# Where the memory's product is read out of PSUM, and when a group's result is split, in an attention and mixture-of-experts kernel

## The chip, the core and the metric

The kernel runs on one core of a Trainium2 chip. The metric is the device time of one execution in microseconds (us). A core has five engines that run their own instruction streams and meet only at semaphores: TensorE (PE, with its weight loads shown as PEld), VectorE (DVE), ScalarE (ACT), GpSimd (POOL) and SyncE (SP, which here only issues transfers). Each engine works through its stream strictly in order.

## The reference

Three stages follow each other. The first is causal attention mixed with a linear memory, for 2 batches, 8 heads, 576 positions and 64 columns a head:

```
local   = softmax(q k' / 8, causal) v
phi(x)  = where(x > 0, x, exp(x) - 1) + 1
mem_out = (phi(q) M_prev) / (phi(q) z_prev + 1e-6)
attn    = g * mem_out + (1 - g) * local          # g = sigmoid(beta), one number a head
```

The second is a gated feed-forward layer, `(silu(x w_gate) * (x w_val)) w_out`, with 1152 tokens, 512 columns and 1536 inner columns. The third routes each token to one of 8 experts by the largest logit and puts it through that expert's two matrices with a ReLU between them. Everything is float32.

## The kernel before

**Precision.** Large products are made of three TensorE passes: each operand is kept as a high part (type fp32r, a copy with fewer bits) and a low part (the operand minus the high part). For the attention's result y, the high part `xh` is a cast by ScalarE and the low part `xl` a subtraction by GpSimd.

**Attention in 16 groups.** A group is one batch, one half of the positions (the first 256 or the last 320) and one pair of heads. In this text they are numbered 0 to 15 in the order in which they run: 0 to 3 are the first halves of batch 0, 4 to 7 its second halves, 8 to 15 the same for batch 1. A group has 2 or 3 units, each of 128 (or 64) query rows; there are 40 units. For a unit TensorE makes the scores (`emit_s`, into a PSUM tile of tag `s`), VectorE takes the row maximum (`emit_max`), ScalarE the exponentials P with their sums (`emit_exp`), TensorE transposes P (`emit_t`, tiles `tp`), ScalarE copies the transposes to SBUF (`PT`), and TensorE multiplies them with v into the group's PSUM tile `u` (`emit_av`).

**The end of a group** is in `emit_av` (lines 315 to 334). The weights of the softmax, (1 - g) over its sums, come from GpSimd as `rb`, are transposed into a PSUM tile `tr` and copied by ScalarE to `R` (line 275). TensorE makes the memory's product `mo` (line 329) from `ph`, which already holds g phi(q) over its norm. Then VectorE multiplies u with R (line 331) and adds mo, read from PSUM (line 332), ScalarE casts the sum to `xh` (line 333), and GpSimd subtracts for `xl` (line 334).

**Order.** The program is written out by hand: unit k+3 has its scores made while unit k is transposed and unit k-1 multiplied with v. One round of that is three ticks, 3k, 3k+1 and 3k+2; `emit_av` for a unit u runs in tick 3u+5. Other work hangs on ticks in a table (`at_tick`, run by `do`): loads, the phi(q) steps (`phi_exp`, `phi_sum`, `phi_norm`, `phi_t`), the scaling of q (lines 116 and 118), the repacking of the weights from 64-bit words (`narrow`, lines 422 to 427). From the fifth group on, after each tick a part of the feed-forward layer's first products is put in (`up`, tiles `gv`, line 492), with its weight splits (`wh` by ScalarE, line 453; `wl` by VectorE or GpSimd, line 456). That work fills TensorE where attention would leave it waiting.

**PSUM.** Three banks of tag `m` go round in turn among `tp`, `tr`, `tphi` (the transposes of phi(q)), `gv` and `mo` (the function `bank`). The fourth tile after `tr`, `mo` or any of them waits until the last reader of the first one is done.

Of the kernel before, what the change touches and what calls it, by code (L numbers as in the profile page):

```python
# [8 lines left out]
F32 = mybir.dt.float32  # L9
# [10 lines left out]
B, H, S, D = 2, 8, 576, 64  # L20
# [25 lines left out]
def tile_attention_moe(  # L46
# [18 lines left out]
    nc = tc.nc  # L65
# [4 lines left out]
    def pool(name, side=None, **kw):  # L70
        st = ExitStack()
        if side:
            kw["side"] = side
        return st.enter_context(tc.tile_pool(name=name, bufs=1, **kw)), st
# [8 lines left out]
    def bank(name):  # L83
        return psb.tile([128, 512], F32, tag="m", bufs=3, name=name)
# [5 lines left out]
    at, at_st = pool("at", "right")  # L90


    HALF = 256
# [3 lines left out]
    def cols(n):  # L97

        e = groups[n][1]
        return (HALF, S - HALF, S) if e else (0, HALF, HALF)  # L100
# [87 lines left out]
    NU = len(units)  # L188
# [14 lines left out]
    def emit_s(u):  # L203
        n, i = units[u]
        o, m = QT[i]
        w = o + m
        s = psa.tile([128, 2, 512], F32, tag="s", bufs=2, name="s")
        s_t[u] = s
        heads = [op_t[n][64 * h:64 * h + 64] for h in range(2)]
        if i < 4:  # L210
            for h, t in enumerate(heads):
                nc.tensor.matmul(s[:, h, 0:w], lhsT=t[:, 0, o:w], rhs=t[:, 1, 0:w], start=True, stop=False)  # L212
            for h in range(2):
                nc.tensor.matmul(s[:, h, o:w], lhsT=identb, rhs=maskb, start=False, stop=True)  # L214
        else:
            c = S // 2
            for a in range(2):
                for h, t in enumerate(heads):
                    nc.tensor.matmul(s[64 * h:64 * h + 64, a, 0:c], lhsT=t[:, 0, o:w], rhs=t[:, 1, a * c:a * c + c],
                                     start=True, stop=(a == 0), skip_group_check=True)  # L220
            nc.tensor.matmul(s[:, 1, c - 64:c], lhsT=identb, rhs=maskb2, start=False, stop=True, skip_group_check=True)
# [3 lines left out]
    def emit_max(u):  # L225
        n, i = units[u]
        P = at.tile([128, 2, 512], F32, tag="P", bufs=T["Pb"], name="P")
        st = at.tile([128, 2], F32, tag="st", bufs=5, name="st")
        sv, vs = views(u, s_t[u], P)
        k = len(vs)  # L230
        nc.vector.tensor_reduce(out=st[:, 0:k], in_=sv, axis=AX.X if k == 2 else AX.XY, op=ALU.max, negate=True)  # L231
        p_t[u] = (P, st, vs)
# [11 lines left out]
    def last_of(u):  # L244
        return u + 1 == NU or units[u + 1][0] != units[u][0]

    def emit_norm(u):

        if not last_of(u):
            return  # L250
        n, i = units[u]
        b, e, p = groups[n]
        k = 4 + e
        sm = sum_t.pop(n)[:, 0:k]
        nc.vector.tensor_scalar(sm, sm, 1e-9, None, op0=ALU.add)
        nc.vector.reciprocal(sm, sm)
        rb = r_t[n] = at.tile([128, 5, 64], F32, tag="rb", bufs=2, name="rb")
        nc.gpsimd.tensor_tensor(out=rb[:, 0:k], in0=sm.unsqueeze(2).to_broadcast([128, k, 64]),
                                in1=omgs[:, p, 0:k].unsqueeze(2).to_broadcast([128, k, 64]), op=ALU.mult)

    def emit_r(n):

        b, e, p = groups[n]
        rb, gw = r_t[n], cols(n)[1]
        t = bank("tr")
        for x in range(2):
            nc.tensor.transpose(out=t[:, 128 * x:128 * x + 128], in_=rb[:, 2 * x:2 * x + 2].rearrange("p a d -> p (a d)"),
                                identity=ident)
        if e:
            for h in range(2):  # L270
                hs_ = slice(64 * h, 64 * h + 64)
                nc.tensor.matmul(t[hs_, 256:320], lhsT=rb[hs_, 4], rhs=ident[hs_, hs_], start=True, stop=True,
                                 skip_group_check=True)
        R = r_t[n] = at.tile([128, S - HALF], F32, tag="R", bufs=2, name="R")
        nc.scalar.copy(R[:, 0:gw], t[:, 0:gw])

    def emit_t(u, x):

        n, i = units[u]
        P = p_t[u][0]  # L280
        if x == 0:
            pt_t[u] = at.tile([128, 2, 512], F32, tag="PT", bufs=2, name="PT")
        PT = pt_t[u]
        t = bank("tp")
        mode = T["ev" + str(0 if u < first[NP] else 1 if u < first[2 * NP] else 2)]
        ev = (nc.scalar.copy, nc.vector.tensor_copy)[(x % 2, 0, 1, x % 2 * (u % 2))[mode]]
        tv = t.rearrange("p (j m) -> p j m", m=128)
        if i < 4:
            for j in range(i + 1):
                nc.tensor.transpose(out=tv[:, j, :], in_=P[:, x, j * 128:(j + 1) * 128], identity=ident)  # L290
            ev(PT[:, x, 0:128 * (i + 1)], t[:, 0:128 * (i + 1)])  # L291
        else:
            pf, ptf = (z.rearrange("p a b -> p (a b)") for z in (P, PT))
            for y, j in enumerate(((0, 1, 2), (3, 4))[x]):
                kw = QT[j][1]
                nc.tensor.transpose(out=tv[0:kw, y, :], in_=pf[:, j * 128:j * 128 + kw], identity=ident)
            if x == 0:
                ev(ptf[:, 0:384], t[:, 0:384])
            else:
                ev(ptf[:, 384:512], t[:, 0:128])  # L300
                ev(ptf[0:64, 512:640], t[0:64, 128:256])

    def emit_av(u):
        n, i = units[u]
        vt = v_t[n]
        o, m = QT[i]
        PT = pt_t.pop(u)
        p_t.pop(u)
        ptf = PT.rearrange("p a b -> p (a b)")
        g0, gw, _ = cols(n)  # L310
        if u == first[n]:
            u_t[n] = psb.tile([128, 512], F32, tag="u", bufs=1, name="u")
        U = u_t[n]
        c0 = o - g0
        end = last_of(u)
        if end:
            emit_r(n)
        for j in range(i + 1):
            kw = QT[j][1]
            for h in range(2):  # L320
                rhs = PT[:, h, j * m:j * m + m] if i < 4 else ptf[0:kw, j * 128 + 64 * h:j * 128 + 64 * h + 64]
                nc.tensor.matmul(U[64 * h:64 * h + 64, c0:c0 + m], lhsT=vt[0:kw, j, 64 * h:64 * h + 64],  # L322
                                 rhs=rhs, start=(j == 0 and u == first[n]), stop=(end and j == i), skip_group_check=True)
        if end:
            b, e, p = groups[n]
            zt, mt, ph = batch_t[b]
            U, gs = u_t.pop(n)[:, 0:gw], slice(g0, g0 + gw)
            M = bank("mo")[:, 0:gw]
            nc.tensor.matmul(M, lhsT=mt[:, p, :], rhs=ph[e][:, p, :], start=True, stop=True)
            y = at.tile([128, S - HALF], F32, tag="y", bufs=2, name="y")[:, 0:gw]  # L330
            nc.vector.tensor_mul(y, U, r_t.pop(n)[:, 0:gw])  # L331
            nc.vector.tensor_add(y, M, y)  # L332
            nc.scalar.copy(xh[b][:, p, gs], y)
            nc.gpsimd.tensor_sub(xl[b][:, p, gs], y, xh[b][:, p, gs].bitcast(F32))

    chores = {}

    def at_tick(t, fn, *args):
        chores.setdefault(t, []).append((fn, args))

    def do(t):
        for fn, args in chores.pop(t, ()):
            fn(*args)
# [22 lines left out]
    def attn():  # L366
        for t in range(min(chores), -3 * LA):
            do(t)
        for k in range(-LA, NU + 1):
            do(3 * k)  # L370
            if k + LA < NU:
                emit_s(k + LA)
                emit_max(k + LA)
            if 0 <= k < NU:
                emit_t(k, 0)
            yield 3 * k
            do(3 * k + 1)
            if 0 <= k + LA - 1 < NU:
                emit_norm(k + LA - 1)
            if k + LA < NU:  # L380
                emit_exp(k + LA)
            if 0 <= k < NU:
                emit_t(k, 1)
            yield 3 * k + 1
            do(3 * k + 2)
            if 0 <= k - 1:
                emit_av(k - 1)
            yield 3 * k + 2


    WN = 2 * KC * 128
# [9 lines left out]
    for k, f in enumerate(seq):  # L401
        if f not in hold:
# [3 lines left out]
            y = max((y for y in range(RS) if k == 0 or hold[y] != seq[k - 1]), key=later)  # L406
# [114 lines left out]
    xh = [xw.tile([128, KC, S], F32R, name=f"xh{b}") for b in range(B)]  # L521
    xl = [xw.tile([128, KC, S], F32R, name=f"xl{b}") for b in range(B)]
# [83 lines left out]
    def bank2(name):  # L606
        return psc.tile([128, 512], F32, tag="c", bufs=4, name=name)
# [253 lines left out]
    for t in range(NT):  # L861
# [4 lines left out]
        y = bank2("y")  # L866
# [352 lines left out]
```

## Time and profile before

| | us |
|---|---|
| Runs of the kernel | 551.59, 553.46, 553.57 (median 553.46) |
| Profiled execution | 554.45 |
| Its span, first to last instruction | 552.7 |
| TensorE busy in the span | 520.3 (94%) |
| VectorE busy | 360.9 (65%) |
| ScalarE busy | 278.8 (50%) |
| GpSimd busy | 195.7 (35%) |

Attention with its filling takes the first 222 us or so of the span, the rest of the gated layer and the routing the stretch to about 400 us, and the experts what follows. TensorE's granted clock is full throughout. The share of busy time of an engine is a mean over these stages, so the rows below are cut by stretch. A busy TensorE is not TensorE at its peak, since its ends are modelled; its idle time is what the argument uses.

### The profile page before, as it was taken

How to read it: one execution, taken by the hardware profiler on the slowest of the kernel's cores; microseconds unless marked ns; L12 is line 12 of the kernel's file. 1: busy time of each engine (PE TensorE's matmuls, PEld its weight loads, DVE VectorE, ACT ScalarE, POOL GpSimd, SP SyncE). 2: the span in 40 equal slices, each digit the busy share in tenths (PEclk: the TensorE clock that was granted, in tenths of full speed). 3: DMA queues.
4: the chain of work that ended last, by engine and by line, in shares of the span. 5: the costliest groups of instructions: out<-in, count | busy, mean ns of one | idle time of the engine just before them, and what ended most of it. 6: DMA issues, size and time to landing. Idle time of an engine off the chain costs nothing. (4 is left out here: it accounts for less than half of the span.)

```text
span 552.7 us, 9638 instructions
## 1 busy us (share of the span) xinstructions
PE 520.3 (94%) x3497; PEld 428.4 (78%) x3497; DVE 360.9 (65%) x718; ACT 278.8 (50%) x623; POOL 195.7 (35%) x231
## 2 busy tenths in 40 slices
PE   4889998999989999999999999999989999989995
PEld 2545776887767889999999887778767979878774
DVE  5786877467876632687877486976688571818161
ACT  5668665565645542333353234434698553626361
POOL 3756356445632211222223475863323111010310
PEclk9999999999999999999999999999999999999999
DMA  8677383318640110699981325255699773554520
GB/s 271 225 244 251 134 268 132 94 49 297 207 157 2 39 39 2 180 283 283 275 256 36 120 74 232 95 156 175 219 341 339 281 254 138 167 211 162 189 90 6
DMA packets 43005, 96.33 MB, mean 174 GB/s; under 512 B 4598, under 2 KB 15350, under 8 KB 41408
## 3 DMA queue, kind: packets, MB, share of 16 engines
q1 hardware_dynamic: 41184, 91.04, 50.6%
q0 software_dynamic: 1760, 4.50, 2.2%
q8 instruction: 36, 0.59, 0.4%
q14 instruction: 25, 0.20, 0.1%
HBM read 78.68 MB, written 17.72 MB: 174 GB/s over the span
## 5 line engine op out<-in xcount | busy, mean ns | idle before, releaser
L492 PE MATMUL gv<-xh,wh 128*128 128x256 f32 (+1 forms) x384 | 122.6, 319 | 1.1 <-ACT PT L291 0.9
L492 PE MATMUL gv<-xh,wl 128*128 128x256 f32 (+1 forms) x384 | 113.8, 296 | 0.7 <-POOL wl L456 0.4
L492 PE MATMUL gv<-xl,wh 128*128 128x256 f32 (+1 forms) x384 | 113.5, 295 | 0.0
L492 PEld LDWEIGHTS gv<-xh,wh 128*128 128x128 f32 x384 | 72.7, 189 | 5.5 <-issue 3.1
L492 PEld LDWEIGHTS gv<-xh,wl 128*128 128x128 f32 x384 | 72.6, 189 | 1.3 <-POOL wl L456 0.8
L492 PEld LDWEIGHTS gv<-xl,wh 128*128 128x128 f32 x384 | 72.9, 190 | 0.7
L456 POOL TENSOR_TENSOR wl<-wf,wh 128x512 fp32r<-128x512 f32 x27 | 40.0, 1481 | 76.1 <-ACT wh L453 76.1
L1087 POOL DMA_INDIRECT out_dram<-hT,gi x13 | 15.5, 1191 | 121.9 <-ACT hT L1086 97.4
L231 DVE TENSOR_REDUCE st<-s 128x2 f32<-128x256 f32 (+4 forms) x40 | 32.2, 806 | 22.3 <-PE s L214 18.2
L241 ACT ACTIVATE P<-s,st 128x128 f32<-128x128 f32 (+4 forms) x72 | 39.2, 551 | 10.3 <-DVE st L231 9.9
L508 DVE SCALAR_TENSOR_TENSOR th<-th,gv 128x256 f32<-128x256 f32 (+1 forms) x48 | 21.7, 451 | 33.4 <-ACT th L507 33.3
L869 PE MATMUL y<-wo_h,hh 128*128 128x512 f32 x108 | 43.2, 400 | 0.0
L730 DVE SCALAR_TENSOR_TENSOR prod<-y,wrb 128x512 f32<-128x512 f32 x56 | 34.8, 686 | 11.9 <-ACT xr L727 11.9
L869 PE MATMUL y<-wo_h,hl 128*128 128x512 f32 x108 | 42.4, 392 | 0.0
L869 PE MATMUL y<-wo_l,hh 128*128 128x512 f32 x108 | 42.4, 392 | 0.0
L453 ACT CAST wh<-wf 128x512 fp32r<-128x512 f32 x54 | 33.6, 622 | 15.4 <-DMA wf<-wsp 15.4
L291 ACT COPY PT<-tp 128x128 f32<-128x128 f32 (+3 forms) x64 | 27.2, 426 | 27.9 <-PE tp L290 27.9
L212 PE MATMUL s<-qk 64*128 64x128 f32 (+3 forms) x128 | 28.5, 524 | 8.0 <-ACT qk L116 7.8
L1067 DVE SCALAR_TENSOR_TENSOR hcl<-w,hch 128x288 fp32r<-128x288 f32 x24 | 11.0, 457 | 35.5 <-ACT hch L1066 35.5
L322 PE MATMUL u<-PT,vt 128*64 128x128 f32 (+1 forms) x480 | 32.8, 269 | 0.3 <-DVE y L331 0.3
L630 POOL TENSOR_TENSOR hl<-hT,hh 128x512 fp32r<-128x512 f32 (+1 forms) x27 | 30.9, 1176 | 3.3 <-ACT hh L628 3.3
L290 PE MATMUL tp<-ident,P 128*128 128x128 f32 x160 | 28.1, 284 | 3.5 <-DVE y L332 1.4
(381 smaller groups left out, 1260.0 us busy)
## 6 DMA issues: line engine op xcount, KB each, us to landing
hT<-in_w_dram SPq DMA_DIRECT2D x64, 512.0 KB, 5.7
wr<-in_wgv_dram SPq DMA_DIRECT2D x12, 1024.0 KB, 5.9
wf<-wsp SPq DMA_DIRECT2D x15, 512.0 KB, 6.6
wor<-in_w_out_dram SPq DMA_DIRECT2D x12, 512.0 KB, 4.5
wsp<-wf SPq DMA_DIRECT2D x10, 512.0 KB, 6.7
disp<-pad SPq DMA_DIRECT2D x16, 257.0 KB, 7.0
xd<-disp SPq DMA_DIRECT2D x14, 257.0 KB, 6.4
qk<-in_qk_dram SPq DMA_DIRECT2D x8, 320.0 KB, 4.3
```

What stands on the lines that cost most here:

```text
L212: nc.tensor.matmul(s[:, h, 0:w], lhsT=t[:, 0, o:w], rhs=t[:, 1, 0:w], start=True, stop=False)
L231: nc.vector.tensor_reduce(out=st[:, 0:k], in_=sv, axis=AX.X if k == 2 else AX.XY, op=ALU.max, negate=True)
L241: nc.scalar.activation(o, a, AF.Exp, bias=st[:, x:x + 1], accum_out=sum_t[n][:, c + x:c + x + 1])
L290: nc.tensor.transpose(out=tv[:, j, :], in_=P[:, x, j * 128:(j + 1) * 128], identity=ident)
L291: ev(PT[:, x, 0:128 * (i + 1)], t[:, 0:128 * (i + 1)])
L322: nc.tensor.matmul(U[64 * h:64 * h + 64, c0:c0 + m], lhsT=vt[0:kw, j, 64 * h:64 * h + 64], rhs=rhs, start=(j == 0 and u == first[n]), stop ...
L453: nc.scalar.copy(hi[:, sl], w[:, sl])
L456: (nc.gpsimd if pool_ else nc.vector).tensor_sub(lo[:, sl], w[:, sl], hi[:, sl].bitcast(F32))
L492: nc.tensor.matmul(a, lhsT=wt[:, s, c, :], rhs=xt[b][:, c, sl], start=(c == 0 and y == 0), stop=(c == KC - 1 and y == 2))
L630: (nc.gpsimd if t else nc.vector).tensor_sub(hl[:, fs, d], src, hh[:, fs, d].bitcast(F32))
L730: nc.vector.scalar_tensor_tensor(out=prod[e % 2], in0=y, scalar=1.0, in1=wrb[e], op0=ALU.mult, op1=ALU.mult, accum_out=lg[:, e:e + 1])
L869: nc.tensor.matmul(y, lhsT=a[:, k, :], rhs=w[:, k, :], start=st, stop=en)
```

## The change

ScalarE copies `mo` from PSUM to a new SBUF tile `Ms` (two buffers) right behind the product, and VectorE's addition reads `Ms` in place of the PSUM tile. The cast to `xh` and the subtraction for `xl` leave `emit_av` and become a function of their own, `emit_xs`, hung on the table at the next tick, 3u+6. A last call of `do` runs that of the last group.

```
             M = bank("mo")[:, 0:gw]
             nc.tensor.matmul(M, lhsT=mt[:, p, :], rhs=ph[e][:, p, :], start=True, stop=True)
+            Ms = at.tile([128, S - HALF], F32, tag="Ms", bufs=2, name="Ms")[:, 0:gw]
+            nc.scalar.copy(Ms, M)
             y = at.tile([128, S - HALF], F32, tag="y", bufs=2, name="y")[:, 0:gw]
             nc.vector.tensor_mul(y, U, r_t.pop(n)[:, 0:gw])
-            nc.vector.tensor_add(y, M, y)
-            nc.scalar.copy(xh[b][:, p, gs], y)
-            nc.gpsimd.tensor_sub(xl[b][:, p, gs], y, xh[b][:, p, gs].bitcast(F32))
+            nc.vector.tensor_add(y, Ms, y)
+            at_tick(3 * u + 6, emit_xs, b, p, gs, y)
+
+    def emit_xs(b, p, gs, y):
+
+        nc.scalar.copy(xh[b][:, p, gs], y)
+        nc.gpsimd.tensor_sub(xl[b][:, p, gs], y, xh[b][:, p, gs].bitcast(F32))
...
             yield 3 * k + 2
+        do(3 * NU + 3)
```

The lines of the changed kernel behind this place stand up to 7 higher than before (453 is 460 there). The orders of TensorE, VectorE and SyncE are the same as before; those of ScalarE and GpSimd change. In the pieces below a number behind a name is the program's buffer: 86 is batch 0's `xh`, 81 and 84 are weight buffers.

ScalarE's stream at the end of group 6, before:

```order
L275 COPY R<-tr 128x320
L333 CAST xh_86<-y 128x320
L453 CAST wh_84<-wf_81 128x512
L151 ACTIVATE pe<-px 128x512
L152 ACTIVATE px<-px 128x512
L291 COPY PT<-tp 128x512
```

and of the changed kernel at the same place:

```order
L275 COPY R<-tr 128x320
L331 COPY Ms<-mo 128x320
L460 CAST wh_84<-wf_81 128x512
L151 ACTIVATE pe<-px 128x512
L152 ACTIVATE px<-px 128x512
L339 CAST xh_86<-y 128x320
L291 COPY PT<-tp 128x512
```

The cast to `xh` has moved behind a weight split and both phi(q) activations, and still stands ahead of the copy of the next transposes. Groups 5, 9, 11, 14 and 15 move it behind one or two other instructions in the same way.

ScalarE's stream at the end of group 0, before:

```order
L275 COPY R<-tr 128x256
L333 CAST xh_86<-y 128x256
L291 COPY PT<-tp 128x256
L241 ACTIVATE P,sums<-s,st 128x128 x2
L291 COPY PT<-tp 128x256
```

and of the changed kernel:

```order
L275 COPY R<-tr 128x256
L331 COPY Ms<-mo 128x256
L339 CAST xh_86<-y 128x256
L291 COPY PT<-tp 128x256
L241 ACTIVATE P,sums<-s,st 128x128 x2
```

Here nothing is written between the two ticks, so the cast stays where it was, behind the new copy. That is so in 10 of the 16 groups.

## Rows read from the trace of the kernel before

**Rows 1.** Busy time in stretches: stretch, length, then each engine's busy us (instructions)
```profile
30.00:45.00 15.00, 12.25 (x86) 6.41 (x84) 12.78 (x22) 10.27 (x30) 10.14 (x8) 1.00 0.70 223
...
60.00:75.00 15.00, 15.00 (x136) 11.69 (x138) 11.37 (x18) 8.09 (x22) 6.16 (x5) 1.00 0.66 209
75.00:90.00 15.00, 13.55 (x134) 10.85 (x131) 13.56 (x23) 8.79 (x25) 8.31 (x6) 1.00 0.60 216
...
165.00:225.00 60.00, 59.98 (x534) 51.34 (x532) 25.97 (x47) 25.49 (x66) 11.76 (x14) 1.00 0.10 33
```

**Rows 2.** TensorE's waits, 0 to 225: who for whom, us, times, longest
```profile
PE tp L290 <- DVE y L332: 1.4, 1, 1.4
...
PE tp L296 <- DVE hT L513: 1.0, 1, 1.0
...
PE gv L492 <- ACT PT L291: 0.9, 1, 0.9
PE tphi L180 <- DVE y L332: 0.8, 2, 0.5
```

**Rows 3.** ScalarE's waits, 0 to 225, the one for the addition
```profile
ACT xh L333 <- DVE y L332: 25.6, 16, 4.1
```

**Rows 4.** Lines 332, 275 and 456: durations in ns, min/median/max
```profile
L332 DVE TENSOR_TENSOR y<-mo,y x16: 425/458/493, 24.9 to 219.9; 128x256 f32<-128x256 f32 x8, 128x320 f32<-128x320 f32 x8
...
L275 ACT COPY R<-tr x16: 373/412/463, 22.4 to 218.3; 128x256 f32<-128x256 f32 x8, 128x320 f32<-128x320 f32 x8
...
L456 DVE TENSOR_TENSOR wl<-wf,wh x27: 674/684/1529, 48.2 to 292.6; 128x512 fp32r<-128x512 f32 x27
```

**Rows 5.** Timeline at the end of group 6: start, us, engine, line, [idle before, releaser]
```profile
84.27 0.43 ACT L275 COPY R<-tr 128x320 f32<-128x320 f32 x1
85.03 0.81 PE L329 MATMUL mo<-ph,mt 128*128 128x320 f32 x2
...
86.92 1.77 POOL L170 TENSOR_TENSOR px<-px,nm 128x512 f32<-128x512 f32 x1 [2.86 <-DVE sums L256]
...
88.29 0.49 DVE L332 TENSOR_TENSOR y<-mo,y 128x320 f32<-128x320 f32 x1
...
88.81 0.46 ACT L333 CAST xh<-y 128x320 fp32r<-128x320 f32 x1 [4.12 <-DVE y L332]
88.84 0.66 PE L290 MATMUL tp<-ident,P 128*128 128x128 f32 x4 [1.45 <-DVE y L332]
...
90.90 0.57 ACT L291 COPY PT<-tp 128x512 f32<-128x512 f32 x1
...
91.52 0.39 PE L492 MATMUL gv<-xh,wh 128*128 128x256 f32 x1 [0.87 <-ACT PT L291]
```

**Rows 6.** Timeline: a VectorE split of weights beside a GpSimd product
```profile
97.49 1.04 POOL L170 TENSOR_TENSOR px<-px,nm 128x512 f32<-128x512 f32 x1 [0.60 <-DVE sums L255]
97.55 1.52 DVE L456 TENSOR_TENSOR wl<-wf,wh 128x512 fp32r<-128x512 f32 x1
```

**Rows 7.** Timeline: the additions of groups 0, 1 and 3, and GpSimd beside them
```profile
23.44 1.89 POOL L170 TENSOR_TENSOR px<-px,nm 128x512 f32<-128x512 f32 x1 [0.62 <-DVE nm L168]
24.86 0.42 DVE L332 TENSOR_TENSOR y<-mo,y 128x256 f32<-128x256 f32 x1
...
28.97 2.18 POOL L159 TENSOR_TENSOR pe<-px,zt 128x512 f32<-128x512 f32 x1 [1.33 <-DVE px L158]
30.46 0.42 DVE L332 TENSOR_TENSOR y<-mo,y 128x256 f32<-128x256 f32 x1
...
45.05 1.26 POOL L159 TENSOR_TENSOR pe<-px,zt 64x512 f32<-64x512 f32 x1
45.56 0.42 DVE L332 TENSOR_TENSOR y<-mo,y 128x256 f32<-128x256 f32 x1
```

**Rows 8.** Timeline at the end of group 11, and VectorE's next recorded idle
```profile
148.16 0.70 PE L329 MATMUL mo<-ph,mt 128*128 128x256 f32 x2
148.50 1.29 POOL L456 TENSOR_TENSOR wl<-wf,wh 128x512 fp32r<-128x512 f32 x1
148.90 0.42 DVE L332 TENSOR_TENSOR y<-mo,y 128x256 f32<-128x256 f32 x1
...
161.69 0.42 DVE L508 SCALAR_TENSOR_TENSOR th<-th,gv 128x256 f32<-128x256 f32 x1 [1.49 <-ACT th L507]
```

## The prediction
> **What bounds the kernel now.** I read the busy time by stretch first, then TensorE's waits, then ScalarE's, then the timeline at the places that these name. The stretches [rows 1] show TensorE without idle from 60 to 75 us and all but without it from 165 to 225 us (59.98 of 60): there the filling covers whatever the other engines do. It has idle time in two kinds of places: in the first groups, which have no filling yet (12.25 of 15 us busy from 30 to 45, with VectorE busier than TensorE at 12.78), and where VectorE is full (75 to 90: VectorE 13.56, TensorE 13.55). What the change can give is TensorE's idle time that comes from a group's end, and that is little: 1.4 us of waits for the addition at a transpose, 0.8 us in two pieces at `tphi`, and 0.9 us of a wait for a PT copy [rows 2], together 3.1 us of 552.7. ScalarE's wait for the addition is far larger, 25.6 us over the 16 groups [rows 3], but ScalarE is not what the end waits for in the filled stretches; most of those microseconds buy nothing.
>
> **The copy of mo.** It adds 16 instructions to ScalarE. Their nearest row is the copy of `tr` to R, of the same shapes: 373 to 463 ns, median 412 [rows 4], so 16 x 0.41 = 6.6 us of work in all. Each falls into the time in which ScalarE waited for the addition, 25.6 / 16 = 1.6 us a group, so I cost the work itself at 0; if that cover were gone in the five unfilled groups, it would be 5 x 0.41 = 2.1 us. The copy waits for TensorE's `mo`, and behind it in ScalarE's stream stand the cast or the next split and PT copies; none of these could pass the cast before either.
>
> **The bank.** `mo` is now released by the copy rather than by the addition. At group 6 that counts [rows 5]. The product ends at 85.03 + 0.81 = 85.84, ScalarE has been free since 84.70, so the copy ends near 86.3. TensorE reached the next transpose at 88.84 - 1.45 = 87.39 and finds the bank free: 1.45 us gained. What is late next is the PT copy: it stood at 90.90 behind the cast, a split and two activations. The last three now run ahead of the cast, which can go when the addition is done. Below I put the addition's end at 89.18; then the cast ends near 89.65, the PT copy near 90.3, and the `gv` product that began at 91.52 begins near 90.3. Taken: -1.2 us. Ends: -2.3 (both waits, 1.45 + 0.87, gone) and 0. At groups 1 and 3 TensorE gets the 0.8 us of [rows 2] at `tphi` back, but waits soon after for PT copies that stand behind the cast; I put that into the next term's lower end.
>
> **The addition, with both inputs in SBUF.** By itself it should cost the same: a VectorE instruction with two SBUF inputs takes 684 ns for 512 columns at the median, against 425 to 493 ns for 256 and 320 columns with one input in PSUM [rows 4], which is one line of about 1 ns a column with a fixed 0.17 us. But the former has a maximum of 1529 ns, the latter of 493. The long ones lie beside GpSimd: a split issued at 97.55 took 1.52 us where GpSimd worked from 97.49 to 98.53 [rows 6]; 98.53 plus most of 0.68 is the 99.07 at which it ended. So VectorE stood still until GpSimd's instruction was over. The old additions beside GpSimd did not: those of groups 0, 1 and 3 took 0.42 us each [rows 7].
>
> [...]
>
> With that, by the times of the old trace:
> - Group 0: issued at 24.86, GpSimd busy until 25.33: +0.47. Group 1: 30.46 against 31.15: +0.69. Group 3: 45.56 against 46.31: +0.75 [rows 7]. In these groups cast, PT copy and exponentials follow the addition on ScalarE in the old order, and VectorE's next row maximum follows it too, so the ring of engines moves with it. Sum 1.91; I take +1.5, since the earlier release of the bank lets TensorE run 0.8 us ahead in places. Ends: +1.9, and -0.8 if nothing is blocked and the banks count fully.
> - Group 6: issued at 88.29, GpSimd until 88.69, end at 88.69 + 0.49 = 89.18 [rows 5]; that is already in the -1.2.
> - Group 11: the copy cannot end before 148.16 + 0.70 + 0.41 = 149.27, and GpSimd's split runs to 149.79 [rows 8], so the addition ends near 150.2 in place of 149.32. VectorE has no recorded idle time from there to 161.69 [rows 8], and TensorE waits 1.0 us for a VectorE evacuation in this stretch [rows 2]. About half of the 0.9 us is absorbed, since the weight repacking two places on was blocked by GpSimd anyway. Taken +0.5. Ends: 0, and +2.1 if GpSimd's next product goes first, once more 1.26 us.
> - The other groups: the addition starts up to 0.5 us later (`mo` plus copy in place of `mo` alone). In 60 to 75 and 165 to 225 us TensorE has no idle time to lengthen [rows 1]: 0, at most +0.5 together.
>
> **The tick.** ScalarE's stream moves the cast only where something is written between the ticks, in 6 groups of 16; in the others it still waits for the addition right behind the new copy. So most of ScalarE's 25.6 us becomes a shorter wait and a copy. GpSimd's subtraction passes one other instruction in four groups; its result is first read ticks later. 0.
>
> **Sum.** 0 - 1.2 + 1.5 + 0.5 + 0 = +0.8 us on the profiled execution of 554.45, so 555.25. That execution lies 0.99 above the median of the runs, 553.46; against the median the forecast is 554.3. By the ends the sum runs from -0.8 - 2.3 = -3.1 to 1.9 + 0 + 2.1 + 0.5 = +4.5.
>
> **Rivals.**
> [...]
> - *The freed bank and the earlier work on ScalarE set the pace.* All 3.1 us of waits [rows 2] go and none returns: 550.4. Against it: VectorE is full in the very stretches where TensorE waits [rows 1], and it has not a single instruction less.
> [...]
>
> **How the numbers follow.** The forecast has a chance of 0.52, no blocking 0.18, the two larger ones 0.14 (faster) and 0.16 (slower). A measurement of this kernel can tell about 0.5%, or 2.8 us, from no change: 550.7 to 556.2 is "the same". The forecast and the case without blocking lie inside. So faster 0.14, same 0.70, slower 0.16. The range goes from 550.5 to 557.4: the ends of the sum, cut where both large rivals keep part of their chance, with the 1 us by which the runs of before differ from their median already inside it.
>
> **What the changed profile would show.** TensorE's waits no longer name the addition; at group 6 the transpose has no idle time and the `gv` product behind it comes about 1.2 us earlier relative to 84 us. The addition's durations, 425 to 493 ns before, have a maximum near 0.9 to 1.3 us, the long ones beside GpSimd instructions and in groups 0, 1, 3 or 11. ScalarE's wait for the addition falls from 25.6 us to about 13 (less 6.6 for the copies, less about 1 us in each of the 6 moved groups), without the time following. The end of group 4, near 56 us, comes 0 to 2 us later. The forecast is wrong if the additions stay below 0.5 us throughout, if TensorE's idle time before 225 us changes by more than 3 us, or if time moves behind 225 us, where the program is the same.

## The result, and the profile after

The changed kernel takes 554.63 us (median of 21 executions, 550.24 to 558.99) against 551.28 us for the kernel before (21 executions): a ratio of 1.0057, 95% interval 1.0036 to 1.0078, about 3.1 us. One slow execution of the changed kernel, at 558.99 us, is left out of the ratio. The time lies in the predicted range, and the sign is that of the sum (+0.8 us), but the size is not: the loss is just past the 0.5% that was called "the same". That the forecast of 554.3 us lies within 0.4 us of the measured time is luck: it was counted from 553.46 us, the median of three runs, and the kernel before takes 551.28 us here.

The profiled execution took 557.47 us. Its page, span and granted clock in 40 slices:

```profile
span 555.7 us, 9657 instructions
...
PEclk9999998999999999999999999999999999999999
```

One slice fell below 0.9 of the full clock; the profile of before had none. Such drops come and go between executions of either kernel (the mean granted clock of one execution is 0.983 to 1.000 among these 21 of the change, 0.987 to 1.000 among those of the kernel before in the experiments), so the two spans are not to be subtracted.

The additions, which lasted 425 to 493 ns before [rows 4]: minimum, median, maximum, and what VectorE waited for ahead of them.

```profile
L334 DVE TENSOR_TENSOR y<-Ms,y x16: 425/493/1046, 24.2 to 224.4; 128x256 f32<-128x256 f32 x8, 128x320 f32<-128x320 f32 x8
its engine sat idle before it (us, times) until:
  ACT Ms L331: 4.5, 8
```

The three of the first groups, with GpSimd beside them, answer to [rows 7]; start, duration:

```profile
22.82 1.89 POOL L170 TENSOR_TENSOR px<-px,nm 128x512 f32<-128x512 f32 x1 [0.62 <-DVE nm L168]
...
24.25 0.74 DVE L334 TENSOR_TENSOR y<-Ms,y 128x256 f32<-128x256 f32 x1
...
28.67 2.19 POOL L159 TENSOR_TENSOR pe<-px,zt 128x512 f32<-128x512 f32 x1 [1.32 <-DVE px L158]
...
30.16 0.98 DVE L334 TENSOR_TENSOR y<-Ms,y 128x256 f32<-128x256 f32 x1
...
45.28 1.27 POOL L159 TENSOR_TENSOR pe<-px,zt 64x512 f32<-64x512 f32 x1
45.78 1.05 DVE L334 TENSOR_TENSOR y<-Ms,y 128x256 f32<-128x256 f32 x1
```

Each ends 0.28 us behind GpSimd's instruction: 22.82 + 1.89 = 24.71 and 24.99, 30.86 and 31.14, 46.55 and 46.83. I read this as VectorE issuing the addition, standing, and doing it when GpSimd was through. The added 0.32 to 0.63 us stand inside the additions and in no wait for a semaphore, so that here the two engines meet elsewhere than at semaphores. Group 5 (0.77 us), 6 (0.75), 8 (1.02) and 11 (0.76) are long too; the other nine take 0.42 to 0.49 us.

TensorE's and ScalarE's waits up to 225 us, to be held against [rows 2, 3]:

```profile
ACT xh L339 <- DVE y L334: 12.2, 14, 1.8
ACT Ms L331 <- PE mo L329: 10.6, 11, 1.2
...
PE tp L290 <- ACT PT L291: 2.4, 2, 1.3
PE tp L296 <- DVE hT L520: 1.6, 1, 1.6
PE tphi L180 <- ACT PT L291: 1.3, 2, 1.0
PE tp L296 <- ACT PT L291: 1.2, 1, 1.2
```

The addition is gone from TensorE's list, and ScalarE's wait for it has halved; the waits that TensorE now has are for PT copies and for an evacuation by VectorE, 6.5 us in these four rows. At group 6, where the prediction saw the transposes without idle time, they wait for such an evacuation:

```profile
90.25 0.66 PE L290 MATMUL tp<-ident,P 128*128 128x128 f32 x4 [0.86 <-DVE hT L520]
```

To see where the time goes, I measured how long TensorE takes from one group's product `mo` to another's. In the early stretch, groups 0, 1 and 4, before and after:

```profile
22.23 1.20 PE L329 MATMUL mo<-ph,mt 128*128 128x256 f32 x2
...
28.37 0.70 PE L329 MATMUL mo<-ph,mt 128*128 128x256 f32 x2 [0.26 <-ACT PT L291]
...
53.84 0.81 PE L329 MATMUL mo<-ph,mt 128*128 128x320 f32 x2
```

```profile
21.61 1.22 PE L329 MATMUL mo<-ph,mt 128*128 128x256 f32 x2
...
28.07 0.70 PE L329 MATMUL mo<-ph,mt 128*128 128x256 f32 x2 [0.26 <-ACT PT L291]
...
54.70 0.81 PE L329 MATMUL mo<-ph,mt 128*128 128x320 f32 x2
```

Group 0 to group 1 took 6.14 us and takes 6.46: the product of group 1 waits in both for a PT copy, which stands behind the delayed addition's cast on ScalarE. (The version with one SBUF input, below, takes 6.57 us there in its first profile although its additions are short: TensorE's score products in this stretch last up to 1.23 us in place of 0.70. Why is open: the change's profile has such a product there too, at 22.76 us, 0.80 us long in place of 0.49, at a granted clock of 1.00.) Group 1 to group 4 took 25.47 us and takes 26.63. The same reading for all profiles of this study gives a small set of values, because these stretches repeat to 0.02 us as long as the clock stays full (differences of the starts of `mo`, us; stretches with a clock drop in them are left out; where the granted clock of a stretch is not listed, I read a drop from products that last longer than elsewhere, as 1.22 us in place of 0.70):

| Kernel | group 1 to 4 | 6 to 7 | 7 to 10 | 10 to 12 |
|---|---|---|---|---|
| before | 25.47 | 18.03 | 32.12 | 34.29 |
| the change | 26.63 | 17.18 | 32.12 | 35.17 |
| copy alone | | | 32.12 | 35.18 |
| tick alone | 25.75 | 16.95 | 32.12 | 34.28 |
| change, one SBUF input | 25.33 | 16.92 | 32.12 | 34.29 |

A clock drop in the last column's stretch adds 1.5 us: 35.81 in a second profile of the kernel before, 36.71 in the first one of the change. For the change 17.18 comes from its second and third profile (the first had a drop there, 18.74), and 35.17 from its third and from the kernel with late copies (the copy in groups 4 to 15 alone, below). The 25.75 of the tick alone is that of the last version below, which is the same kernel up to group 4 and has no drop there. The copy alone took 19.78 us from group 6 to 7 with a drop in it:

```profile
94.00:96.00 2.00, 2.00 (x18) 1.73 (x13) 1.02 (x2) 0.91 (x3) 0.39 (x1) 0.58 1.01 329
```

With the clock full the change is thus 0.32 + 1.16 - 0.85 + 0.88 = +1.5 us. Two profiles whose clock is full from the product of group 0 to that of group 15 say the same, 219.10 - 22.23 = 196.87 us before and 219.91 - 21.55 = 198.36 in the change's third profile:

```profile
219.10 0.81 PE L329 MATMUL mo<-ph,mt 128*128 128x320 f32 x2
```

```profile
21.55 1.22 PE L329 MATMUL mo<-ph,mt 128*128 128x256 f32 x2
...
219.91 0.81 PE L329 MATMUL mo<-ph,mt 128*128 128x320 f32 x2
```

### The profile page after: what moved, and what is told of

The parts are those of the page before. It is cut to its first block, busy times and chain, and to the rows that moved or that the text cites. A ratio compares the mean times of both kernels' runs of the same rounds, so it can differ in the third digit from the quotient of the medians.

```text
span 555.7 us, 9657 instructions
## 1 busy us (share of the span) xinstructions
PE 525.0 (94%) x3497; PEld 431.5 (78%) x3497; DVE 365.8 (66%) x718; ACT 284.8 (51%) x639; POOL 196.2 (35%) x231
## 5 line engine op out<-in xcount | busy, mean ns | idle before, releaser
L322 PE MATMUL u<-PT,vt 128*64 128x128 f32 (+1 forms) x480 | 34.2, 277 | 0.0
```

## The experiments

A is the theory that the additions' second SBUF input meets GpSimd and delays VectorE, with more stretches of a lower clock behind it. B says that the clock falls as often in the kernel before. C blames ScalarE's extra copies or the later cast. D puts the loss behind the early groups.

**The kernel before, again** (no edit). 

> The unchanged kernel once more, for the granted clock of its single executions. Theory A (the second SBUF input of 16 additions delays VectorE, the longer idle time of TensorE is followed by stretches at half the granted clock): ratio 0.998 to 1.002, and the mean granted clock of its executions lies above that of the changed kernel's (mean there 0.993), at 0.996 to 1.000. Rival B (the clock falls as often in the kernel before; the 3 us are delays of the engines alone): mean clock 0.991 to 0.995 here too. [...]

Ratio 1.0015 (0.9985 to 1.0045); mean clock 0.9936 over its 12 executions, 0.9926 over 29 more of the same kernel run beside them. B was right on this: the clock falls in the kernel before too, and a mean of 1.000 is the exception: none of these 41 executions has it (0.988 to 0.999). In this profile the granted clock was 0.53 from 162 to 165 us, behind the wait beside group 11; and the product `mo` of group 1, at 27.98 us, lasts 1.22 us in place of 0.70.

**The copy alone.**

```
-            at_tick(3 * u + 6, emit_xs, b, p, gs, y)
+            emit_xs(b, p, gs, y)
```

> The copy of mo to SBUF and the addition from there, with the cast and the subtraction left where they were. A: the additions of groups 0, 1, 3 and a few others last 0.7 to 1.1 us, the place of group 4 is reached about 1.5 us later from group 0 on, ratio 1.004 to 1.009. C: if the later cast is what costs, ratio 0.999 to 1.002; if the copies cost, the same 1.004 to 1.009 with additions that need not be long.

1.0096 (1.0061 to 1.0130), above the 1.0057 of the whole change, though the intervals overlap. The additions are those of the change (maximum 1047 ns). Group 6 shows what the missing tick does: TensorE's rows with idle time, and the PT copy, in this kernel,

```profile
90.43 0.66 PE L290 MATMUL tp<-ident,P 128*128 128x128 f32 x4 [0.86 <-DVE hT L520]
...
92.16 0.57 ACT L291 COPY PT<-tp 128x512 f32<-128x512 f32 x1
...
92.78 0.39 PE L499 MATMUL gv<-xh,wh 128*128 128x256 f32 x1 [1.69 <-ACT PT L291]
```

The wait for the addition is gone, as the early release of `mo`'s bank should do, and it buys nothing: the next transpose waits 0.86 us for the evacuation behind the addition, and the product behind it 1.69 us for the PT copy, which stands behind cast, split and two activations as before. Together 2.55 us, against 1.45 + 0.87 = 2.32 before [rows 5], so that with a full clock this stretch would be about 0.2 us longer than before, by an estimate from the waits alone.

**The tick alone.**

```
-            Ms = at.tile([128, S - HALF], F32, tag="Ms", bufs=2, name="Ms")[:, 0:gw]
-            nc.scalar.copy(Ms, M)
...
-            nc.vector.tensor_add(y, Ms, y)
+            nc.vector.tensor_add(y, M, y)
```

(against the changed kernel). 

> The cast and the subtraction one tick later, with mo read from PSUM by the addition as before: no copy. A: additions stay at 0.42 to 0.50 us, ratio 0.996 to 1.001, with group 6 about 0.9 us better since the PT copy stands behind less. C (the later cast costs): ratio 1.003 to 1.006.

1.0006 (0.9981 to 1.0030), additions 424 to 493 ns. At group 6:

```profile
88.56 0.66 PE L290 MATMUL tp<-ident,P 128*128 128x128 f32 x4 [1.45 <-DVE y L332]
...
89.25 0.58 ACT L291 COPY PT<-tp 128x512 f32<-128x512 f32 x1 [0.26 <-PE tp L290]
```

TensorE waits 1.45 us for the addition as before, but the PT copy comes 0.69 us behind the start of the transposes in place of 2.06 (88.84 and 90.90 in [rows 5]), the wait after it is gone, and the stretch is 1.08 us shorter. So the gain at group 6 is the tick's, not the bank's. C falls as to the later cast.

**The change with one SBUF input.**

```
-            nc.vector.tensor_mul(y, U, r_t.pop(n)[:, 0:gw])
-            nc.vector.tensor_add(y, Ms, y)
+            nc.vector.tensor_mul(U, U, r_t.pop(n)[:, 0:gw])
+            nc.vector.tensor_add(y, U, Ms)
```

> The whole change, but VectorE writes the product of u and R back into u's PSUM bank, so that the addition has one input in PSUM and one in SBUF. Copies, order of ScalarE and GpSimd and the early release of mo's bank are those of the changed kernel; u's bank is held until the addition is done. A: additions at 0.42 to 0.50 us, ratio to the kernel before 0.995 to 1.001, 3 us or so under the changed kernel. C: as the changed kernel, 1.004 to 1.007.

0.9986 (0.9959 to 1.0012). Copies, tick and early release are all there; what is gone is the long additions:

```profile
L334 DVE TENSOR_TENSOR y<-u,Ms x16: 424/458/492, 24.3 to 220.5; 128x256 f32<-128x256 f32 x8, 128x320 f32<-128x320 f32 x8
```

A second run, beside the change itself: 

> The change with the product written back into u's bank, again, beside the change itself. A: 0.996 to 1.001, below the change by 2 to 4 us. If it comes out at 1.003 or more, the first run's gain was chance.

1.0002 (0.9986 to 1.0018). Both intervals lie below those of the change (1.0036 to 1.0078, and 1.0056 to 1.0118 in the run beside the second). This is the run that decides: 16 extra copies on ScalarE cost nothing that can be measured, and without the second SBUF input of 16 additions the loss is gone. By the table 1.30 + 0.26 + 0.88 = 2.4 us of it lie in these three stretches. The rest of C falls.

**The two halves, and the change beside them.**

```
-            Ms = at.tile([128, S - HALF], F32, tag="Ms", bufs=2, name="Ms")[:, 0:gw]
-            nc.scalar.copy(Ms, M)
+            Ms = M
+            if n < NP:          # n >= NP in the other half
+                Ms = at.tile([128, S - HALF], F32, tag="Ms", bufs=2, name="Ms")[:, 0:gw]
+                nc.scalar.copy(Ms, M)
```

> The cast a tick later everywhere, the copy of mo and the addition from SBUF in groups 0 to 3 alone. A (the second SBUF input is the cost wherever GpSimd works beside it): the additions of groups 0, 1 and 3 last 0.7 to 1.05 us and the others 0.49 at most; from the product mo of group 1 to that of group 4 it takes 26.6 us in place of 25.5, from group 6 to 7 some 16.9; ratio 1.001 to 1.004. Rival D (the early groups have slack and the loss is made behind them): ratio 0.997 to 1.001.

0.9993 (0.9973 to 1.0012), in the range of D and below that of A. Additions 0.74, 0.97 and 1.04 us in groups 0, 1 and 3, none over 0.49 behind. Group 6 to 7 takes 16.94 us. By the table the early loss, 0.32 + 1.16, and the tick's gain, 1.08, all but cancel, so the ratio does not clear the early additions of a cost. (Group 1 to 4, 26.80 us, has a clock drop in it.)

> The reverse: copy and addition from SBUF in groups 4 to 15 alone. A: groups 0 to 4 as before (25.5 us from mo of group 1 to mo of group 4), long additions at groups 5, 6, 8 and 11, from mo of group 10 to that of group 12 some 0.9 us more than the 34.3 of the kernel before, where no drop of the granted clock lies between; ratio 1.000 to 1.003. D: ratio 1.003 to 1.007.

1.0040 (1.0019 to 1.0062). Long additions at groups 5, 6, 8 and 11 (0.77, 0.75, 1.03, 0.74), group 1 to 4 takes 25.73 (a clock drop near 40 us lies in it, which cost nothing there: 25.75 without one), 6 to 7 17.19, 10 to 12 35.17: at full clock the sum is +0.3 us, and yet it measures 2.2 us. D is right in the ratio, above the 1.003 of A, and A in the places.

> The whole change again, on the same chip as the two halves. A: 1.003 to 1.008, about the sum of the excesses of the two halves.

1.0087 (1.0056 to 1.0118, 6 executions), above the expected range. The two halves' excesses do not add up to it (-0.4 and +2.2 us against 4.8); that each half has the tick's gain in it accounts for about 1 us of the gap. The clock is lower here too, mean 0.9878 against 0.9941 for the kernel before beside it.

**The clock.** 

> The whole change once more, beside executions of the kernel before whose granted clocks are listed. A (delays of the engines, and with them more stretches at half the granted clock): ratio 1.004 to 1.009, and the mean clock of its executions at least 0.002 below that of the kernel before in the same call. B (the clock falls as often before): mean clocks within 0.001 of each other, and the ratio about 1.002, the 1.05 us that the delays of the engines come to by themselves.

1.0043 (1.0022 to 1.0064); mean clock 0.9910 against 0.9938. So ratio and clock come out as A has it. A missing 0.0028 of 551 us would be 1.5 us, which is an upper end: among the executions of one kernel a mean clock lower by 0.001 goes with 0.17 us more (one slope through 99 executions of the kernel before, with a level for each set of executions) to 0.31 us more (38 of the change), not with 0.55. By these slopes it is 0.5 to 0.9 us, and with the 1.5 of the stretches 2.0 to 2.4, against 2.4 measured.

**Group 11 freed.**

```
-            nc.vector.tensor_mul(y, U, r_t.pop(n)[:, 0:gw])
-            nc.vector.tensor_add(y, Ms, y)
+            uR = U if n == 11 else y
+            nc.vector.tensor_mul(uR, U, r_t.pop(n)[:, 0:gw])
+            nc.vector.tensor_add(y, Ms, uR)
```

> The whole change, but in group 11 alone the product of u and R is written back into u's PSUM bank, so that only this addition has one SBUF input. A: from mo of group 10 to mo of group 12 it takes 34.3 us where no clock drop lies between (35.8 with one), in place of 35.2 (36.7); ratio 1.001 to 1.005, some 1 to 2 us under the change. If the early groups and not this place carry the loss: 1.004 to 1.009, as the change.

1.0035 (1.0013 to 1.0057), mean clock 0.9938 as in the kernel before. From group 10 to 12 it takes 34.27 us, so the 0.9 us there is this one addition's. The ratio lies less than 1 us below that of the change, in place of the 1 to 2 us expected, and the intervals overlap. From group 0 to group 15 its profile, with a full clock, takes 219.56 - 22.09 = 197.47 us, 0.6 more than before, while the runs measure 1.9 more with the same mean clock.

**A version against both.** The tick alone, and one GpSimd instruction out of VectorE's way:

```
-            pool_ = x and (c < T["lo0"] if c < XF else c < XF + T["lo1"])
+            pool_ = x and c != 12 and (c < T["lo0"] if c < XF else c < XF + T["lo1"])
```

> The cast a tick later without the copy, and one weight split of GpSimd (the second half of the thirteenth weight block), behind which VectorE's last repacking step stood 3.2 us beside group 11, is given to VectorE. If GpSimd's next instruction does not take its place: VectorE is through 0.6 us earlier, TensorE's wait for the evacuation there falls from 1.0 to about 0.4 us, ratio 0.996 to 0.999. If GpSimd's scaling of q takes its place: no gain, or 0.4 us lost, 0.999 to 1.002.

0.9979 (0.9960 to 0.9998), median 548.92 us: faster than the kernel before by a hair's breadth over the noise, and than the changed one clearly. In the tick-alone kernel VectorE's last repacking step beside group 11 stood behind two GpSimd instructions,

```profile
154.41 1.03 POOL L170 TENSOR_TENSOR px<-px,nm 64x512 f32<-64x512 f32 x1 [3.63 <-DVE nm L168]
154.59 3.17 DVE L432 SCALAR_TENSOR_TENSOR wf<-wr,wf 128x1024 int32<-128x1024 int32 x1
...
155.41 1.27 POOL L461 TENSOR_TENSOR wl<-wf,wh 128x512 fp32r<-128x512 f32 x1
...
158.21 0.44 PE L296 MATMUL tp<-ident,P 128*128 128x128 f32 x2 [1.01 <-DVE hT L518]
```

and here behind one; GpSimd's next instruction, which lasts 1.98 us where the shortest of its shape lasts 1.00, seems to wait for it in turn:

```profile
154.30 1.04 POOL L170 TENSOR_TENSOR px<-px,nm 64x512 f32<-64x512 f32 x1 [3.63 <-DVE nm L168]
154.48 1.94 DVE L432 SCALAR_TENSOR_TENSOR wf<-wr,wf 128x1024 int32<-128x1024 int32 x1
155.31 1.98 POOL L118 TENSOR_SCALAR qk<-qk 128x320 f32<-128x320 f32 x1
156.34 0.93 DVE L461 TENSOR_TENSOR wl<-wf,wh 128x512 fp32r<-128x512 f32 x1
...
157.73 0.44 PE L296 MATMUL tp<-ident,P 128*128 128x128 f32 x2 [0.62 <-DVE hT L518]
```

TensorE waits 0.62 us in place of 1.01, and group 10 to 12 takes 33.96 us in place of 34.28.

## Why the prediction was right, and where not

- **The second SBUF input** was the term that decided, at the places named. The delays at groups 0, 1 and 3 were predicted as 0.47, 0.69 and 0.75 us and are 0.32, 0.56 and 0.63 (0.74, 0.98 and 1.05 less 0.42): I had counted the whole addition behind GpSimd's end, and it ends 0.28 us behind it, not 0.42. By what means an instruction of GpSimd holds up one of VectorE no run shows. What the runs show is that the seven long additions, all with two SBUF inputs, end 0.28 us (256 columns) or 0.35 us (320 columns) behind a GpSimd instruction with two inputs beside them, and that the addition of group 9, beside one with a single input (126.49 us, GpSimd's scaling of q from 125.89 to 126.91), takes 0.43 us. On TensorE the early groups lose 0.32 + 1.16 = 1.5 us, as predicted.
- **The bank.** The sum at group 6 was near (-1.2 predicted, -0.85 measured), and its cause was half wrong. The prediction needed both the freed bank (1.45 us) and the earlier PT copy for it, and booked the gain under the bank, with "0" for the tick. With the bank freed alone TensorE's waits there grow from 2.32 to 2.55 us; with the tick alone the stretch is 1.08 us shorter. The three banks go round, so the transposes and products behind take the next wait in place of the one removed. The step that failed is "the tick: 0": by itself it gives all of the gain, and the freed bank none.
- **Group 11** was mis-sized: +0.5 predicted, +0.88 measured. I had let half of the delay vanish because VectorE's next repacking step was blocked anyway. It is not absorbed. Before, that step ended 0.56 us behind one GpSimd instruction, and the subtraction for `xl` came after it:

```profile
149.75 1.26 POOL L159 TENSOR_TENSOR pe<-px,zt 64x512 f32<-64x512 f32 x1
149.82 1.75 DVE L422 TENSOR_SCALAR wf<-wr 128x1024 int32<-128x1024 int32 x1
...
150.98 1.18 POOL L334 TENSOR_TENSOR xl<-y,xh 128x256 fp32r<-128x256 f32 x1
```

In the change it starts later and ends 0.55 us behind the subtraction, which now goes first:

```profile
151.29 1.46 POOL L159 TENSOR_TENSOR pe<-px,zt 64x512 f32<-64x512 f32 x1
...
151.94 2.05 DVE L429 TENSOR_SCALAR wf<-wr 128x1024 int32<-128x1024 int32 x1
...
152.71 0.73 POOL L340 TENSOR_TENSOR xl<-y,xh 128x256 fp32r<-128x256 f32 x1
```

- **The other groups at 0** held, but the prediction had missed two places there. Its terms cost the additions of groups 0, 1, 3, 6 and 11; in the trace of before those of group 5 (at 70.56 us, GpSimd busy from 70.15 to 71.44) and group 8 (at 113.93, GpSimd from 113.64 to 114.93) lie beside a GpSimd instruction too, and both became long. They cost nothing: group 4 to 6 takes 31.19 us before and 31.17 in the change, group 7 to 10 takes 32.12 us in all kernels. TensorE had work there.
- **ScalarE's copies at 0** held (change with one SBUF input), and ScalarE's wait for the addition fell to 12.2 us (13 predicted) without the time following.
- **The size.** In the stretches the change costs 1.5 us at full clock, against the +0.8 of the sum: the bank's term gave 0.35 us less than taken, group 11 cost 0.4 us more. But three measurements gave 3.1, 4.8 and 2.4, so part of the loss lies in what no term held. Some of it goes with the granted clock. In the two measurements with clocks of both kernels on one chip, the change's mean is lower by 0.0063 and 0.0028; by the slopes above that is 1.1 to 2.0 and 0.5 to 0.9 us. In the first, the change's mean clock was 0.9932, inside the 0.9926 to 0.9941 of the kernel before in the later ones (the clocks of the kernel before beside it are not on record), so there the clock hardly accounts for the loss. Kernels whose later additions have one SBUF input were within 0.0012 of the kernel before; those whose have two were lower by 0.0018 to 0.0063, but for the one with group 11 freed (0.0000), which still lost 1.9 us. That idle time at group 11 causes the drops is not shown: a drop near 160 us stands in two of the five profiles whose addition there is long and in two of the eight where it is short. So up to about 2 us of the change's loss stays open. The part behind the product of group 15, where the program is the same, takes 328.9 to 333.6 us in the profiles, in no order of the kernels, so a loss of 1 or 2 us there can be neither found nor ruled out.

## What to carry to other kernels

Before a VectorE operand is moved from PSUM to SBUF to free a bank, look at which GpSimd instructions run beside it: here a second SBUF input made seven of 16 additions wait for them (0.74 to 1.05 us in place of 0.42 to 0.49). A freed bank is worth only what the next wait behind it leaves; the order of ScalarE's stream, which all of them feed, was worth more here (1.08 us at group 6 by the PT copy's place in it). And compare a change of 1 us by stretches of the trace that repeat, not by two spans.

## What the runs showed of the hardware that was not expected

TensorE's granted clock falls to 0.50 for some microseconds in some executions and not in others, behind the same idle time of 1.59 us. The change's first profile, in stretches (length, busy us of each engine, granted clock, DMA):

```profile
160.00:162.00 2.00, 0.44 (x4) 0.23 (x2) 2.00 (x3) 0.81 (x2) 2.00 (x2) 1.00 0.00 0
162.00:164.00 2.00, 1.29 (x10) 1.09 (x11) 0.64 (x1) 1.33 (x5) 0.44 (x1) 1.00 0.73 115
164.00:166.00 2.00, 2.00 (x20) 1.74 (x19) 1.62 (x3) 0.47 (x2) 0.00 (x0) 0.58 0.89 303
166.00:168.00 2.00, 2.00 (x10) 1.64 (x10) 0.00 (x0) 0.00 (x0) 0.00 (x0) 0.57 0.87 350
```

TensorE had just waited 1.59 us for VectorE's evacuation, and was busy again when the clock fell: by half microseconds it was 0.81 from 164.0, 0.50 from 164.5 to 167.5, 0.78 behind that and 1.00 from 168.0. In the kernel with late copies the same wait,

```profile
159.65 0.44 PE L296 MATMUL tp<-ident,P 128*128 128x128 f32 x2 [1.59 <-DVE hT L522]
```

was followed by a full clock:

```profile
162.00:164.00 2.00, 2.00 (x24) 1.70 (x26) 1.38 (x3) 0.36 (x1) 0.00 (x0) 1.00 0.93 340
164.00:166.00 2.00, 2.00 (x16) 1.46 (x14) 1.02 (x2) 0.63 (x2) 0.00 (x0) 1.00 0.73 299
```

One such drop costs 1.5 us here (35.81 against 34.29 from group 10 to 12), and it hit four of the 13 profiles of this study at this place, one of them of the kernel before and one of the version with one SBUF input. Near 40 us one cost nothing where the cast comes a tick later (25.73 us against 25.75 from group 1 to 4, with six transposes that last 1.49 us in place of 0.83). So a drop can follow an idle stretch of 1.59 us and need not; what decides it is not shown.
